# Moving transposes from TensorE to DMA in an attention and mixture-of-adapters kernel

## The chip, the cores and the metric

The kernel runs on one core of one Trainium2 chip. The metric is the device time of one execution in microseconds (us). Of three runs the median was 380.7 us (380.69 to 381.25).

## The reference

Four images of 12,288 query rows attend to a pooled and projected key/value set of 768 rows each (a 4 x 4 mean over a 384 x 32 grid). The output of the attention, 49,152 rows of 128, goes through a mixture of eight rank-16 adapters of which each row takes the best two.

```python
kv_pool = kv.reshape(B, H // r, r, W // r, r, C).mean(axis=(2, 4))
k = v = kv_pool.reshape(B, -1, C) @ w_sr
a = softmax(q @ k.T / sqrt(C))
x = (a @ v).reshape(-1, 128)
logits = x @ w_gate                  # 8 per row, the two largest are kept
w = softmax(the two largest)
out = x + sum over the two e of w[e] * (x @ A[e]) @ B[e]
```

## The kernel before, in words

**Chunks and slots.** The rows are cut into 96 chunks of 512 (24 to a batch). A chunk has six key tiles of 128 keys. Its life: `scores` (line 286) makes three units of two key tiles, each two 512-column matmuls into PSUM (`sg`, two buffers) and one exp on ScalarE into `em` (line 294). `attend` (line 296) multiplies `em` with the values, 24 matmuls into `acc`. `normalize` (line 313) divides on VectorE and leaves the rows x in `xn` (line 320). `top` and `route` (lines 335, 344) find the two best adapters, the latter on GpSimd, mostly for two chunks at once; `gates` (line 363) makes their weights with a tanh on ScalarE. `down` (line 412) multiplies the transposed x with all A, `gate` (line 417) weights the result into `hg` on VectorE, `up` (line 426) multiplies the transposed hg with all B, and `finish` (line 431) adds x and sends the output from SyncE's queue.

A slot is one turn of the loop at line 547. In slot k the scores of chunk k are made, chunk k-1 is attended, chunk k-2 is normalized, and older chunks go through down, gate and up. Everything is recorded in program order by `keep`, so that each engine, and SyncE's queue of DMAs, takes its instructions in the order of the source.

**Two ways of transposing.** `transposes` (line 371) uses TensorE: four 128 x 128 transposes of x, four of hg, into a PSUM bank `tt_ps`, then a copy to `tts` on VectorE (line 389). For chunks 68 to 89 (`by_dma`, line 328) it is done by DMA: `narrow` (line 402) copies x as bf16 into a strip on GpSimd, `gate` writes hg into the other half of the strip, and `turn_dma` (line 405) transposes both halves with one DMA inside SBUF from SyncE's queue. A chunk turned that way has two slots of flight. The strips lie in a tile of the pool of key rows that is free by then.

**The other DMAs.** q is cast to bf16 by a DMA from DRAM to DRAM on GpSimd's queue (`cast_q`, line 78) and then transposed by DMA from DRAM to SBUF on SyncE's queue (`load_qT`, line 83), 2048 rows at a time. `load_kv` (line 95) loads the rows of the next batch's key tiles, twelve DMAs of 512 KB to a batch, one in each of the first twelve slots of a batch. The additions that pool them run on GpSimd (line 223, 1.27 us each), three at a time in every second slot; nine steps `keys`, `values` and `turn` (from line 233) then make the keys and values on TensorE and VectorE. `begin` (line 468) issues the DMAs of a slot.

Of the kernel before, what the change touches and what calls it, by code (L numbers as in the profile page):

```python
# [20 lines left out]
def kernel(  # L21
# [33 lines left out]
    ppool = ctx.enter_context(tc.tile_pool(name="ppool", bufs=8))  # L55
# [20 lines left out]
    q_bf, qT, kvr, spare = {}, {}, {}, {}  # L76
# [6 lines left out]
    def load_qT(g):  # L83
        if g < B * NG - GC:
            t = qpool.tile([P, GT], BF16, tag="qT", name="qT")
        else:
            if "q" not in spare:
                spare["q"] = kvpool.tile([P, 4, 2, 4 * C], FP32, tag="kvr", name="qTs")
            t = spare["q"][:, g % GC].rearrange("p x c -> p (x c)").bitcast(BF16)
        keep(nc.sync.dma_start(t.rearrange("c (j p) -> c j p", p=P),  # L90
                               q_bf[g].rearrange("(p j) c -> p (j c)", p=P), transpose=True))
        qT[g] = t
# [109 lines left out]

    ring = [xpool.tile([P, 2, S, C + E], FP32, tag=f"xr{i}", name="xn") for i in range(6)]
# [82 lines left out]
    def scores(k, r):  # L286
        b = k // NB
        if k not in em:
            em[k] = ppool.tile([P, J, T], FP16, tag="em", name="em")
# [36 lines left out]
    SOLO, TURN = NCHUNK - 6, NCHUNK - 28  # L326
    sizes = [1, 1] + [2] * (TURN // 2 - 1) + [1] * (NCHUNK - TURN)
    by_dma = range(TURN, SOLO)
    first, size = {}, {}
# [65 lines left out]
    def strip(t, i):  # L395
        if "t" not in spare:
            t_ = kvpool.tile([P, 4, 2, 4 * C], FP32, tag="kvr", name="turn")
            spare["t"] = t_.rearrange("p r x c -> p (r x c)").bitcast(BF16).rearrange(
                "p (n t h s c) -> p n t h s c", n=4, t=2, h=2, s=S)
        return spare["t"][:, t % 4, i]  # L400
# [4 lines left out]
    def turn_dma(t, *what):  # L405
        lo, hi = (0 if what[0][0] is xT or len(what) == 2 else 1), (2 if what[-1][0] is hgT else 1)
        keep(nc.sync.dma_start(strip(t, 1)[:, lo:hi].rearrange("c h s p -> c (h s) p"),
                               strip(t, 0)[:, lo:hi].rearrange("p h s c -> p (h s c)"), transpose=True))
        for i, (d, k) in enumerate(what):
            d[k] = strip(t, 1)[:, lo + i]  # L410
# [52 lines left out]
    casts = sorted([k for k in range(8, 61, GC)] + [15, 19, 23, 39, 43, 47])  # L463
    loads = {4 * g - 6: g for g in range(4, 18)}
    loads.update({61: 20, 63: 21, 64: 18, 65: 22, 66: 19, 67: 23})
    assert len(casts) == B * NG - 4

    def begin(k):
        nonlocal sums, rest
        b, i = divmod(k, NB)  # L470
        g = k // GC
        if k in loads:
            load_qT(loads[k])
        if k in casts:
            cast_q(4 + casts.index(k))
        if b + 1 < B:
            lo = 3 if b == 0 else 0
            if i == lo:
                sums, rest = prepare(b + 1, nc.gpsimd)
                sums = sum(sums, [])  # L480
            if lo <= i < 12 + lo:
                load_kv(b + 1, (i - lo) // 4, (i - lo) % 4, None)
        if k == 7:
            for _ in range(2):
                sums.pop(0)()
# [10 lines left out]
    ready = {k: normed[first[k] + size[k] - 1] + 1 + (k in by_dma[:-1]) for k in range(NCHUNK)}  # L496
    enter, t, left = {}, 1, list(range(NCHUNK - 3))
    while left:
        can = [k for k in left if ready[k] <= t]
        enter[t] = can[:2] if t == SOLO + 2 else can[:1]  # L500
        left = [k for k in left if k not in enter[t]]
        t += 1
# [44 lines left out]
    for k in range(k1, NCHUNK):  # L547
        b, i = divmod(k, NB)
        ka = att.get(k, [])
        kx = enter.get(k, [])  # L550
        begin(k)
# [6 lines left out]
        kn = [n for n in att.get(k - 1, []) if normed[n] == k]  # L558
        unit()
        if kx and not kd and all(x_ in by_dma for x_ in kx):  # L560
            down(kx[0])
            todo = []
            for n in kn:
                normalize(n)
                if n in by_dma:
                    narrow(n, k)
                    todo = [(xT, n)]
            tanhs()
            for h_ in kh:
                if h_ not in by_dma:  # L570
                    transposes(None, h_, nc.vector)
# [3 lines left out]
            if len(kx) == 1:  # L575
                turn_dma(k, *todo)
            for u_ in ku:
                up(u_)
                finish(u_)
            attend(ka[0], 0)  # L580
            attend(ka[0], 1)
            unit()
            for n in kn:
                after_norm(n)
            attend(ka[0], 2)
            for x_ in kx[1:]:
                down(x_)
                gate(x_, strip(k, 0)[:, 0])
                turn_dma(k, (hgT, x_), *todo)
            attend(ka[0], 3)  # L590
            kh, ku = kx, kh
            continue
        tanhs()
        for x_ in kd:
            down(x_)
        for n in kn:
            normalize(n)
            if n in by_dma:
                narrow(n, k)
                turn_dma(k, (xT, n))  # L600
        px, ph = ([c for c in ks if c not in by_dma] for ks in (kx, kh))
        pairs = [(px[j] if j < len(px) else None, ph[j] if j < len(ph) else None)
                 for j in range(max(len(px), len(ph)))]
        for x_, h_ in pairs[:1]:
            transposes(x_, h_, nc.vector)
        for x_ in kd:
            gate(x_)
        unit()
        for u_ in ku:
            up(u_)  # L610
            finish(u_)
        for a_ in ka[:-1]:
            for s in range(S):
                attend(a_, s)
            normalize(a_)
            after_norm(a_)
        if ka and len(ka) == 1:
            attend(ka[0], 0)
        for n in kn:
            after_norm(n)  # L620
        if k >= 13:
            unit()
            n0 = 1
        else:
            attend(ka[0], 1)
            n0 = 2
        for x_ in kx[:1]:
            down(x_)
            gate(x_)
        kd = []  # L630
        if rest and i in ((14, 15, 16, 18, 19, 20, 21, 22, 23) if b == 0 else (11, 12, 13, 17, 18, 19, 21, 22, 23)):
            rest.pop(0)()
        for a_ in ka[-1:]:
            for s in range(n0 if len(ka) == 1 else 0, S):
                if s == S - 1:
                    for x_, h_ in pairs[1:]:
                        transposes(x_, h_, nc.scalar)
                        kd = [x_] if x_ is not None else []
                attend(a_, s)
        ku = kh  # L640
        kh = kx[:1] + kdone
        kdone = kd
        if b + 1 < B and i % 2 == 0 and (8 if b == 0 else 6) <= i <= 20:
            for _ in range(4 if (b, i) == (0, 18) else 3):
                sums.pop(0)()
# [185 lines left out]
```

## Time and profile before

| what | value |
|---|---|
| profiled execution, time | 380.87 us |
| its span | 379.1 us |
| mean granted clock of TensorE | 0.995 |
| instructions | 11473 |
| DMA packets, bytes | 93863, 82.22 MB |
| share of the 16 DMA engines' span, queue of SyncE (q1) | 69.8% |
| outputs: DMAs, size, median to landing | 94, 256 KB, 4.3 us |
| key rows | 45, 512 KB, 7.8 us |
| casts of q | 22, 512 KB, 7.7 us |
| turns of x and hg | 23, 3.1 us |
| transposes of q | 18, 7.4 us (and 4 more into another tile, 6.6 us) |

The page gives the busy time of each engine (PE is TensorE's matmuls, PEld its weight loads, DVE is VectorE, ACT ScalarE, POOL GpSimd, SP SyncE), then the span in 40 slices with a digit for the busy tenths, then the DMA queues, then the chain of work that ended last. Matmuls are pipelined, so the durations of single ones overlap, and sums over groups of them are more than their time.

### The profile page before, as it was taken

What the parts mean: (1) busy time and instruction counts of PE and PEld (TensorE: products, weight loads), DVE (VectorE), ACT (ScalarE), POOL (GpSimd) and SP (SyncE); (2) the same over time, 40 slices, a digit from 0 to 9 for tenths busy, and PEclk for the clock granted to TensorE, in tenths of its full rate; (3) what the DMA queues carried; (4) which work ended last, traced back from release to release, by engine and by line L of the source; (5) the groups of instructions that cost most, each with busy time, mean ns of one, the idle gap of its engine ahead of it and who ended that gap; (6) DMA issues with size and microseconds to landing.
All of it is one profiled execution on the core that took longest, in us unless ns stands there. A gap on an engine that the chain in (4) does not pass through costs nothing.

```text
span 379.1 us, 11473 instructions
## 1 busy us (share of the span) xinstructions
PE 368.8 (97%) x4448; PEld 292.5 (77%) x4448; DVE 307.6 (81%) x925; ACT 293.3 (77%) x368; POOL 217.8 (57%) x493
## 2 busy tenths in 40 slices
PE   8899999999999999999999999999999999999993
PEld 5577788788788887878788887878787777777782
DVE  1447799998989889898989888898988777777785
ACT  1448986776878788787878787777778999999873
POOL 0120468878732387777833267777675666666442
PEclk9999999999999999999999999999999999999998
DMA  7988979999999998997898998989955867777623
GB/s 247 388 291 151 279 184 266 340 224 241 152 213 228 299 278 268 255 235 165 171 201 226 288 239 245 306 233 198 217 137 140 169 163 153 150 205 168 141 86 140
DMA packets 93863, 82.22 MB, mean 217 GB/s; under 512 B 73104, under 2 KB 73872, under 8 KB 93456
## 3 DMA queue, kind: packets, MB, share of 16 engines
q1 hardware_dynamic: 92672, 69.75, 69.8%
q0 software_dynamic: 704, 11.54, 17.0%
q8 instruction: 35, 0.57, 0.6%
q10 hardware_dynamic: 432, 0.20, 0.2%
q14 instruction: 20, 0.16, 0.2%
HBM read 50.53 MB, written 36.70 MB: 230 GB/s over the span
## 4 chain that ended last, share of the span: by engine, by line
PE 91%; DMA 4%; DVE 2%; issue 1%; ACT 1%; SPq 0%; POOL 0%; ACTq 0%; DVEq 0%; POOLq 0%
PE acc L69 35%; PE sg L69 32%; PE tt_ps L69 8%; PE d_ps L69 5%; PE h_ps L69 5%; DMA kvr<-in_kv_dram 4%; PE kpT_ps L69 2%; PE v_ps L69 1%; DVE kvr L135 1%; DVE xn L320 1%; PE kfT_ps L69 1%; DMA out_dram<-osb 1%; PE qT_ps L69 0%; SPq L102 0%; PE tail_ps L69 0%
## 5 line engine op out<-in xcount | busy, mean ns | idle before, releaser
L294 ACT ACTIVATE em<-sg 128x1024 f16<-128x1024 f32 x288 | 282.4, 1022 | 66.8 <-PE sg L69 64.1
L69 PE MATMUL acc<-vx,em 128*128 128x136 f16 x2280 | 166.5, 223 | 0.0
L69 PEld LDWEIGHTS <-em 128*128 128x128 f16 x2304 | 145.2, 98 | 7.7 <-DVE xn L320 0.4
L69 PE MATMUL sg<-qT,kfT 128*128 128x512 bf16 x480 | 142.1, 379 | 0.8 <-ACT em L294 0.7
L320 DVE TENSOR_TENSOR xn<-acc,rinv 128x540 f32<-128x540 f32 x95 | 68.4, 720 | 3.3
L69 PEld LDWEIGHTS <-tts 128*128 128x128 bf16 x564 | 43.0, 98 | 31.6 <-issue 0.4
L223 POOL TENSOR_TENSOR kvr<-kvr 128x512 f32<-128x512 f32 x54 | 67.3, 1270 | 0.1
L352 POOL TENSOR_TENSOR over<-xn,srt 128x64 f32<-128x64 f32 (+1 forms) x120 | 30.9, 278 | 55.4 <-DVE srt L340 55.3
L433 DVE TENSOR_TENSOR osb<-d_ps,xn 128x512 f32<-128x512 f32 x91 | 62.5, 688 | 0.0
L420 DVE TENSOR_TENSOR hg<-h_ps,gw 128x512 bf16<-128x512 f32 x71 | 49.0, 691 | 6.3 <-POOL gw L368 1.2
L389 DVE COPY tts<-tt_ps 128x1024 bf16<-128x1024 bf16 (+1 forms) x73 | 49.0, 672 | 0.0
L69 PEld LDWEIGHTS <-kfT 128*128 128x128 bf16 x576 | 45.3, 98 | 2.7 <-issue 1.0
L315 DVE RECIPROCAL rinv<-acc 128x4 f32<-128x4 f32 x95 | 17.3, 182 | 36.9 <-PE acc L69 35.9
L367 POOL TENSOR_TENSOR gw<-th,over 128x64 f32<-128x64 f32 (+1 forms) x60 | 17.3, 288 | 49.6 <-ACT th L365 47.4
L69 PEld LDWEIGHTS <-xn 128*128 128x128 bf16 x296 | 22.5, 98 | 16.7 <-DVE xn L320 0.4
L340 DVE MAX8 srt<-xn 128x8 f32<-128x8 f32 x380 | 34.4, 152 | 0.1
L69 PE MATMUL sg<-qTs,kfT 128*128 128x512 bf16 x96 | 28.6, 379 | 0.0
L69 PE MATMUL tt_ps<-id_bf,xn 128*128 128x128 bf16 x284 | 27.4, 219 | 0.0
L69 PE MATMUL h_ps<-a_bf,tts 128*128 128x128 bf16 x284 | 27.4, 219 | 0.0
L69 PE MATMUL tt_ps<-id_bf,hg 128*128 128x128 bf16 x280 | 27.1, 219 | 0.0
L69 PE MATMUL d_ps<-b_bf,tts 128*128 128x128 bf16 x276 | 26.7, 219 | 0.1
L358 POOL TENSOR_SCALAR over<-over 128x64 f32<-128x64 f32 (+1 forms) x60 | 19.8, 330 | 5.4
(93 smaller groups left out, 280.7 us busy)
## 6 DMA issues: line engine op xcount, KB each, us to landing
out_dram<-osb SPq DMA_DIRECT2D x94, 256.0 KB, 4.3
kvr<-in_kv_dram SPq DMA_DIRECT2D x45, 512.0 KB, 7.8
qbf<-in_q_dram POOLq DMA_DIRECT2D x22, 512.0 KB, 7.7
qf<-in_q_dram SPq DMA_DIRECT2D x8, 256.0 KB, 7.4
kvr<-in_kv_dram SPq DMA_DIRECT2D x6, 256.0 KB, 7.8
out_dram<-osb SPq DMA_DIRECT2D x3, 128.0 KB, 2.3
turn<-turn SPq DMA_TRANSPOSE x23, 3.1
qT<-qbf SPq DMA_TRANSPOSE x18, 7.4
```

Source lines behind the costliest of these rows:

```text
L69: return keep(nc.tensor.matmul(*a, **k))
L223: keep(adder.tensor_tensor(u[:, lo:hi], u[:, lo:hi], v[:, lo:hi], op=ALU.add))
L294: keep(nc.scalar.activation(em[k][:, 2 * r:2 * r + 2], ps, AF.Exp, bias=0.0, scale=scale))
L315: keep(nc.vector.reciprocal(ri, acc[k][:, :, VC]))
L320: keep(nc.vector.tensor_tensor(x[:, :, 0:VC], acc[k][:, :, 0:VC], ri.unsqueeze(2).broadcast_to([P, S, VC]), op=ALU.mult))
L340: keep(nc.vector.max(srt[k0][:, m, s], xn[k][:, s, C:C + E]))
L352: keep(eng.tensor_tensor(d, lg, so[:, :, i].unsqueeze(2).broadcast_to([P, n, 8]), op=ALU.subtract))
L358: keep(eng.tensor_scalar(mask, mask, 0.0, None, op0=ALU.is_ge))
L367: keep(eng.tensor_tensor(w[:, 0:n], th, mask, op=ALU.mult))
L389: keep(nc.vector.tensor_copy(sb[:, lo:hi], ps[:, lo:hi]))
L420: keep(nc.vector.tensor_tensor(hg[k].rearrange("p s (e r) -> p (s e) r", e=E), hp[k].rearrange("p s (e r) -> p (s e) r", e=E), gw[k0][:, m ...
L433: keep(nc.vector.tensor_tensor(osb, dp[k], xn[k][:, :, 0:C], op=ALU.add))
```

## The change

`by_dma` now begins at chunk 12 instead of 68. From there on hg is always transposed by DMA. x is transposed by DMA for chunks 20, 22, ... 60 and for 62 to 89; for chunks 12 to 19 and the odd ones from 21 to 61 (`x_by_pe`) it is still done on TensorE, one slot before it is used (`turn_next`), with the copy on ScalarE for chunks 13, 17, 21, ... 61 and on VectorE for the others. A chunk under 80 enters `down` five slots after its own slot and `up` three slots after that (three slots of flight), later ones as before (two slots). Pairs of chunks are routed together up to chunk 79 instead of 67.

The tiles of `em` are eight fixed ones; from chunk 13 on only the first four are used for `em`, and the strips lie in the other four: four strips as source, eight as destination. The key rows of batches 2 and 3 are loaded one in every second slot, their additions run one in each slot over 24 slots, and the steps that make keys and values follow behind them. Casts and transposes of q have new slots.

```diff
-    ppool = ctx.enter_context(tc.tile_pool(name="ppool", bufs=8))
...
     def load_qT(g):
-        if g < B * NG - GC:
-            t = qpool.tile([P, GT], BF16, tag="qT", name="qT")
-        else:
-            if "q" not in spare:
-                spare["q"] = kvpool.tile([P, 4, 2, 4 * C], FP32, tag="kvr", name="qTs")
-            t = spare["q"][:, g % GC].rearrange("p x c -> p (x c)").bitcast(BF16)
+        t = qpool.tile([P, GT], BF16, tag="qT", name="qT")
...
+    ems = [xpool.tile([P, J, T], FP16, tag=f"em{i}", name="em") for i in range(8)]
...
-            em[k] = ppool.tile([P, J, T], FP16, tag="em", name="em")
+            em[k] = ems[k % 8 if k < TURN + 1 else k % 4]
...
-    SOLO, TURN = NCHUNK - 6, NCHUNK - 28
-    sizes = [1, 1] + [2] * (TURN // 2 - 1) + [1] * (NCHUNK - TURN)
+    SOLO, TURN, NEAR = NCHUNK - 6, 12, NCHUNK - 16
+    sizes = [1, 1] + [2] * (NEAR // 2 - 1) + [1] * (NCHUNK - NEAR)
     by_dma = range(TURN, SOLO)
+    x_by_pe = [*range(TURN, 20), *range(21, NEAR - 18, 2)]
...
     def strip(t, i):
-        if "t" not in spare:
-            t_ = kvpool.tile([P, 4, 2, 4 * C], FP32, tag="kvr", name="turn")
...
+        n = 4 + t % 8 if i else t % 4
+        v = ems[4 + n // 3].rearrange("p j t -> p (j t)").bitcast(BF16)
+        return v[:, n % 3 * 2 * T:(n % 3 + 1) * 2 * T].rearrange("p (h s c) -> p h s c", h=2, s=S)
...
-    def turn_dma(t, *what):
-        lo, hi = (0 if what[0][0] is xT or len(what) == 2 else 1), (2 if what[-1][0] is hgT else 1)
-        keep(nc.sync.dma_start(strip(t, 1)[:, lo:hi].rearrange("c h s p -> c (h s) p"),
+    def turn_dma(t, u, *what):
+        lo = 0 if what[0][0] is xT else 1
+        hi = lo + len(what)
+        keep(nc.sync.dma_start(strip(u, 1)[:, lo:hi].rearrange("c h s p -> c (h s) p"),
                                strip(t, 0)[:, lo:hi].rearrange("p h s c -> p (h s c)"), transpose=True))
...
-    casts = sorted([k for k in range(8, 61, GC)] + [15, 19, 23, 39, 43, 47])
-    loads = {4 * g - 6: g for g in range(4, 18)}
-    loads.update({61: 20, 63: 21, 64: 18, 65: 22, 66: 19, 67: 23})
+    casts = {4 * g - 8: g for g in range(4, 19)}
+    casts.update({67: 19, 70: 20, 73: 21, 76: 22, 79: 23})
+    loads = {4 * g - 5: g for g in range(4, 20)}
+    loads.update({74: 20, 77: 21, 80: 22, 82: 23})
+    rows_at = {3 + n: (1, n) for n in range(12)}
+    rows_at.update({NB * b - 32 + 2 * n: (b, n) for b in (2, 3) for n in range(12)})
+    adds_at = {7: 2, 8: 3, 10: 3, 12: 3, 14: 3, 16: 3, 18: 4, 20: 3}
+    adds_at.update({k: 1 for k in range(NB - 3, 3 * NB - 3)})
+    keys_at = [14, 15, 16, 18, 19, 20, 22, 23, 23] + [
+        NB * b - 24 + n for b in (2, 3) for n in (5, 6, 7, 13, 14, 15, 21, 22, 23)]
...
-    ready = {k: normed[first[k] + size[k] - 1] + 1 + (k in by_dma[:-1]) for k in range(NCHUNK)}
...
+    enter, ups = {}, {}
+    for k in range(NCHUNK - 3):
+        slow = 1 if k < NEAR else 0
+        if k not in by_dma:
+            t = max(normed[first[k] + size[k] - 1] + 1, max(enter, default=0) + 1 if k < TURN else 0)
+        else:
+            t = min(k + 4 + slow, SOLO + 2)
+            ups.setdefault(t + 2 + slow, []).append(k)
+        enter.setdefault(t, []).append(k)
...
+        def new_x(n):
+            normalize(n)
+            if n in by_dma and n not in x_by_pe:
+                narrow(n, k)
+                return [(xT, n)]
+            return []
+
+        def turn_next(k):
+            for x_ in enter.get(k + 1, []):
+                if x_ in x_by_pe:
+                    transposes(x_, None, nc.scalar if x_ % 4 == 1 else nc.vector)
+
         unit()
-        if kx and not kd and all(x_ in by_dma for x_ in kx):
+        if kx and kx[0] in by_dma:
             down(kx[0])
-            todo = []
-            for n in kn:
-                normalize(n)
-                if n in by_dma:
-                    narrow(n, k)
-                    todo = [(xT, n)]
+            todo = new_x(kn)
             tanhs()
             for h_ in kh:
-                if h_ not in by_dma:
-                    transposes(None, h_, nc.vector)
+                transposes(None, h_, nc.vector)
             unit()
             gate(kx[0], strip(k, 0)[:, 1])
             todo.append((hgT, kx[0]))
-            if len(kx) == 1:
-                turn_dma(k, *todo)
-            for u_ in ku:
+            turn_dma(k, k, *todo)
+            for u_ in ku + ups.get(k, []):
                 up(u_)
                 finish(u_)
-            attend(ka[0], 0)
-            attend(ka[0], 1)
+            attend(ka, 0)
+            attend(ka, 1)
+            turn_next(k)
             unit()
-            for n in kn:
-                after_norm(n)
-            attend(ka[0], 2)
+            after_norm(kn)
+            for _ in range(keys_at.count(k)):
+                rest.pop(0)()
+            attend(ka, 2)
             for x_ in kx[1:]:
                 down(x_)
-                gate(x_, strip(k, 0)[:, 0])
-                turn_dma(k, (hgT, x_), *todo)
-            attend(ka[0], 3)
+                gate(x_, strip(k + 2, 0)[:, 1])
+                turn_dma(k + 2, k + 4, (hgT, x_))
+            attend(ka, 3)
...
+        add(k)
```

## The prediction

> **What bounds the kernel now.** I read the page's busy row and slices first, then the chain, then the DMA queues, then single slots. One slot is one chunk's turn through the loop (lines 547 to 645).
>
> ```profile
> PE 368.8 (97%) x4448; PEld 292.5 (77%) x4448; DVE 307.6 (81%) x925; ACT 293.3 (77%) x368; POOL 217.8 (57%) x493
> PE   8899999999999999999999999999999999999993
> DMA  7988979999999998997898998989955867777623
> PE 91%; DMA 4%; DVE 2%; issue 1%; ACT 1%; SPq 0%; POOL 0%; ACTq 0%; DVEq 0%; POOLq 0%
> q0 software_dynamic: 704, 11.54, 17.0%
> ```
>
> TensorE ends the chain and is full from slice 2 to the end, so every matmul removed is time, until something else is late. The DMA row says what that could be: nearly full up to slice 29 and three quarters after.
>
> The price of a slot is the distance between two reciprocals (line 315, one per chunk). In the timeline of VectorE two plain slots stand 3.61 us apart in the middle, and 3.16 us apart in the late stage where chunks 68 to 89 are already turned by DMA:
>
> ```profile
> 127.56 0.18 DVE L315 RECIPROCAL rinv<-acc 128x4 f32<-128x4 f32 x1 [0.30 <-PE acc L69]
> 131.17 0.18 DVE L315 RECIPROCAL rinv<-acc 128x4 f32<-128x4 f32 x1 [0.38 <-PE acc L69]
> ...
> 320.20 0.18 DVE L315 RECIPROCAL rinv<-acc 128x4 f32<-128x4 f32 x1 [0.75 <-PE acc L69]
> 323.37 0.18 DVE L315 RECIPROCAL rinv<-acc 128x4 f32<-128x4 f32 x1 [0.75 <-PE acc L69]
> ```
>
> The two kinds of slot differ by eight transposes (four of x, four of hg): 0.45 us, so a group of four costs 0.225 us. The late stage also shows the next engine. ScalarE is gapless there, three exps in 3.04 us and a tanh:
>
> ```profile
> 318.51 3.15 ACT L294 ACTIVATE em<-sg 128x1024 f16<-128x1024 f32 x3
> 321.55 0.22 ACT L365 ACTIVATE th<-over 128x32 f32<-128x32 f32 x1
> 321.67 3.15 ACT L294 ACTIVATE em<-sg 128x1024 f16<-128x1024 f32 x3
> ```
>
> **What leaves TensorE.** Chunks 12 to 67 lose their hg group (56). Of x, chunks 20, 22, ... 60 and 62 to 67 are new by DMA (27). That is 83 groups, or 332 matmuls, and the instructions of the changed kernel, listed by engine, have 332 fewer. 83 x 0.225 = 18.7 us; the profiled time 380.87 (span 379.1 and 1.77 around it; the median of the three runs is 380.7) would become **362.2** if nothing else were late. The summed busy time of the two transpose rows would say more, but those durations overlap (219 ns each), so I use the slot distance.
>
> **What the other engines do.** ScalarE per four slots: 12 exps 12.16, two pair tanhs about 0.3, and one copy of a transposed x (13 in all; nearest row 585 ns, line 673) give 13.0 us, against TensorE's 2 x 3.16 + 2 x 3.385 = 13.09. It fits with nothing to spare; the score buffers in PSUM (two) cover the uneven slot. If they don't, 13 x 0.585 = 7.6 us is the most it costs, and a smoother order gains nothing since TensorE stays behind it; I take 0. VectorE does less: its copies of 1024 columns (0.69) shrink to 16 of 512 (0.42). GpSimd gains 27 narrow copies (610 ns, 16.5 us) at 57% busy. Its additions come one per slot at 1.27 us, so a narrow copy can wait for at most one addition, and the DMA behind it is 1.3 us later: inside the slack below. Key rows follow their last addition by half a slot or more; I take 0 for the six groups in batches 2 and 3, at most 1.3 us each if GpSimd slips a slot. The three slots of flight cost nothing on TensorE: they change only which chunk stands in a slot.
>
> **What DMA must carry.** Four views of one microsecond give prices: plain transfers (kv rows, outputs), a transpose inside SBUF, a transpose of q from DRAM, and one that begins badly (two microseconds):
>
> ```profile
> DMA packets 116, 0.39 MB, mean 389 GB/s; under 512 B 8, under 2 KB 8, under 8 KB 116
> ...
> DMA packets 827, 0.21 MB, mean 212 GB/s; under 512 B 827, under 2 KB 827, under 8 KB 827
> ...
> DMA packets 1124, 0.29 MB, mean 288 GB/s; under 512 B 1124, under 2 KB 1124, under 8 KB 1124
> ...
> DMA packets 598, 0.25 MB, mean 127 GB/s; under 512 B 549, under 2 KB 549, under 8 KB 598
> ```
>
> All packets are 256 B in a transpose. So on all 16 engines: an output (0.262 MB at 389 GB/s) 0.67 us; a kv row 1.35; a 128x512 transpose (512 packets at 827 per us) 0.62; a qT (2048 at 1124) 1.82; a cast of q 17.0% x 379.1 / 22 = 2.93.
>
> Slots 22 to 62 of the new order (hg always, x every second, one kv row every second, one qT and one cast every fourth), per four slots: 4 x 0.62 + 2 x 0.62 + 4 x 0.67 + 2 x 1.35 + 1.82 + 2.93 = 13.85, or **3.47 us a slot**. TensorE needs 3.27 a slot there (half at 3.16, half at 3.385), and each key group adds about 0.85 (before, three slots of a group took 3.84, 4.12, 3.72): 41 x 3.27 + 5 x 0.85 = 138.4 us, or 3.38 a slot. DMA is the longer one.
>
> That sum supposes engines that never stand still. How far from it they are is bounded by the kernel before: with a kv row in every slot it carried 0.67 + 1.35 + (1.82 + 2.93) / 4 = 3.21 a slot in 3.61, and TensorE wasn't held up. So the stretch lies between 1.00 and 3.61 / 3.21 = 1.125. The last view above shows where it comes from: 127 GB/s at the start of a transpose. I take the middle, 1.06: two thirds of the new load is of kinds that ran undisturbed in the late stage, one third (qT, cast) of the kind that stretches. 3.47 x 1.06 = 3.68.
>
> Some lag is free. A turn is issued 1.85 us into its slot (320.0 to 321.85), lands 3.1 later, and is now needed 0.43 into the third slot after: 3 x 3.38 + 0.43 - 1.85 - 3.1 = 5.6 us of slack, or 4.3 with a kv row (1.35) queued before it. So slots 22 to 62 take 41 x 3.68 - 4.3 = 146.6, 8.2 more than TensorE's 138.4. Slots 63 to 82 (no kv, x always): (8 x 0.62 + 4 x 0.67 + 1.82 + 2.93) / 4 = 3.10, x 1.06 = 3.29, 65.8 against TensorE's 20 x 3.16 + 0.85 + 0.45 = 64.5: 1.3 more. Behind slot 82 there is slack as before.
>
> Sum: 362.2 + 8.2 + 1.3 = **371.7 us**, faster by 2.4%. With no stretch it is 362.2; with 1.125, 41 x 3.90 - 142.7 = 17.2 and 20 x 3.49 - 64.5 = 5.3 give 384.7.
>
> [...]
>
> **Rivals.**
> 1. *DMA hides it all: 362.2 (chance 0.20 for under 364.5).* For it: 3.47 lies only 0.09 above TensorE's 3.38, and 4.3 us of lag covers 41 x 0.09. Against it: the DMA row is already full at a lower load.
> 2. *Partial: DMA becomes the bound by a little, 364.5 to 380.1 (0.55).* My forecast.
> 3. *Slower: casts on transposes.* [...] Before, transposes were 1.8 of 14.4 us of four slots; now 5.5 of 13.5, and one cast comes in each four. If that brings the stretch over f, with 41 x 3.47 f + 20 x 3.10 f = 204.3 f against 207.2 + 18.7, the gain is eaten at f = 1.106, or **3.84 us a slot**. At 1.125 it is 384.7 (0.20 for over 381.6).
> 4. *SyncE's queue.* It is in order, and a q transpose holds it longest:
>
> ```profile
> 130.26 6.24 SPq L90 DMA_TRANSPOSE qT<-qbf  x1
> 321.85 1.24 SPq L407 DMA_TRANSPOSE turn<-turn  x1
> ```
>
> Per four slots: two turns at 1.24, two of half the size at about 0.62, outputs 4 x 0.53, rows 2 x 0.55, a qT at 6.24, and eleven gaps of 0.09: 14.2, or 3.55 a slot; 41 x 3.55 - 142.7 = 2.9, so 365. It lies inside rival 2.
>
> That the change doesn't move the transposes is excluded by the count of instructions.
>
> **Numbers.** A measurement of this kernel tells about 0.2% from no change. Faster 0.75, within 0.2% 0.05, slower 0.20. The range 361 to 383 leaves out some 0.03 below (a smoother DMA also moves nothing under TensorE's sum) and some 0.13 above.
>
> **What would show it.** Right: slots of about 3.16 and 3.39 in turn where DMA keeps up; TensorE under 95% busy, with waits of h_ps or d_ps matmuls for DMA em<-em in slots 22 to 62, 8 us or so in all; the late stage unchanged at 3.16. Rival 1: TensorE still full, no such waits. Rival 3: these waits over 18 us, turns landing 10 us or more after issue, and mean slots over 3.84. Wrong altogether: ScalarE's copies or GpSimd's additions as the last releaser before TensorE.

## The result, and the profile after

The changed kernel took 420.64 us (median of four runs, 414.91 to 426.52) against 380.98 us (380.69 to 381.35): slower, by a ratio of 1.0916 with a 95% interval of 1.0867 to 1.0965. The ratio lies under that of the medians because two of the four runs of the changed kernel were disturbed and are left out of it. Forecast were 371.7 us and a range of 361 to 383, so it was wrong in size and in sign. The profiled execution took 416.88 us with a span of 415.1.

These lines of the page of the changed kernel answer to those of before: busy time, slices, the chain, two groups of matmuls with the idle time ahead of them (the last two numbers are idle time and its main releaser), and two rows of DMA issues (the last number is the median from issue to landing).

```profile
PE 362.8 (87%) x4116; PEld 278.8 (67%) x4116; DVE 275.2 (66%) x885; ACT 304.7 (73%) x375; POOL 227.0 (55%) x484
...
PE   8899999999989868878799877978886997999993
...
PEclk9999999999999999998979999999998898999998
DMA  8989699999999989999999999999999989986623
...
PE 49%; DMA 28%; POOL 9%; DVE 7%; issue 3%; SPq 1%; ACT 1%; POOLq 0%; DVEq 0%; ACTq 0%
...
L68 PE MATMUL h_ps<-a_bf,em 128*128 128x128 bf16 x196 | 19.5, 223 | 30.0 <-DMA em<-em 30.0
L68 PE MATMUL d_ps<-b_bf,em 128*128 128x128 bf16 x312 | 30.9, 223 | 10.7 <-DMA em<-em 9.9
...
em<-em SPq DMA_TRANSPOSE x78, 4.8
...
qT<-qbf SPq DMA_TRANSPOSE x22, 8.0
```

TensorE is 87% busy after 97%, and works 362.8 us where it worked 368.8. The matmuls h_ps and d_ps, which read what the turns deliver, now wait 39.9 us for a DMA, where the kernel before had no such wait worth a line, and DMA holds 28% of the chain (4% before). The DMA row is full from slice 7 to 34, bar two. The clock row shows 7 or 8 in five slices ahead of the last.

Where the time went, by stages of slots. A stage is the distance between two reciprocals in the timeline of VectorE; the half clock is the time in it for which the trace grants 0.5.

| slots | before | forecast | after | half clock in it |
|---|---|---|---|---|
| 12 to 21 | 37.7 | | 35.8 | 0 |
| 22 to 62 | 152.1 | 146.6 | 175.4 | 10.2 |
| 63 to 82 | 69.6 | 65.8 | 80.9 | 10.2 |
| 83 to 96 | 45.5 | as before | 48.8 | 0 |

Time comes in steps. Two plain slots of 3.61 and 3.62 us and a long one of 9.49, in the timeline of VectorE:

```profile
196.57 0.18 DVE L310 RECIPROCAL rinv<-acc 128x4 f32<-128x4 f32 x1 [0.75 <-PE acc L68]
...
200.18 0.18 DVE L310 RECIPROCAL rinv<-acc 128x4 f32<-128x4 f32 x1 [0.29 <-PE acc L68]
...
203.80 0.18 DVE L310 RECIPROCAL rinv<-acc 128x4 f32<-128x4 f32 x1
...
213.29 0.18 DVE L310 RECIPROCAL rinv<-acc 128x4 f32<-128x4 f32 x1 [1.07 <-PE acc L68]
```

In the long one TensorE stands until a turn has landed. SyncE's queue and TensorE around it (the second number of a line is how long the instruction held its engine; the bracket is the idle time before):

```profile
196.41 4.29 SPq L402 DMA_TRANSPOSE em<-em  x1
200.80 2.29 SPq L429 DMA_DIRECT2D out_dram<-osb  x1
```

```profile
203.60 0.59 PE L68 MATMUL sg<-qT,kfT 128*128 128x512 bf16 x2
207.15 0.61 PE L68 MATMUL h_ps<-a_bf,em 128*128 128x128 bf16 x4 [2.96 <-DMA em<-em]
```

The turn issued at 196.41 landed at 207.1, 10.7 us later. The records of the DMA's packets say what it waited for. A cast begins at 196.84 in 16 packets of 32 KB, which I read as one to an engine. Fifteen end by 200.46; the sixteenth began only at 198.72, took 4.23 us and ended at 202.95. Eight packets of a key row, queued ahead of the turn, then follow one another from 202.93 to 204.19, one at a time (the records don't name engines; one at a time, behind the late packet, I read as that engine). Twenty packets of the turn that began at 202.2 to 202.5, by the same reading on other engines, stand for 1.9 to 2.2 us and end together at 204.42 to 204.45. From 202.5 to 204.2 the DMA view of the profile has next to nothing starting (its first row is in tenths again, for 40 slices of this stretch):

```profile
DMA  0000000000200020020002000200200020002000
...
DMA packets 11, 0.03 MB, mean 19 GB/s; under 512 B 3, under 2 KB 3, under 8 KB 11
```

So, by that reading, the other engines held packets of the transpose and waited for the one that was behind. A second stand, of 1.35 us, follows at 206.0, after a single packet of 16 KB of instructions from 204.87 to 206.01. Behind it comes a loss that the forecast did not have. The windows of the same place (length, busy time of the five engines, then the granted clock, the DMA share and GB/s):

```profile
203.00:207.00 4.00, 1.19 (x15) 0.70 (x12) 1.61 (x4) 1.73 (x2) 1.21 (x1) 0.92 0.96 145
207.00:209.00 2.00, 1.85 (x12) 1.30 (x13) 0.69 (x1) 0.29 (x1) 0.00 (x0) 0.50 0.89 323
...
211.00:213.00 2.00, 2.00 (x16) 1.68 (x15) 0.93 (x6) 1.02 (x1) 1.12 (x4) 0.50 1.23 286
213.00:215.00 2.00, 2.00 (x25) 1.52 (x23) 1.68 (x4) 1.21 (x3) 1.99 (x4) 0.96 0.82 210
```

After its 2.96 us of standing, TensorE runs at half clock for 6.8 us. Such stretches add up to 20.5 us before the tail. An estimate from that, with half the work done at half the clock: they cost at most half of it, 10.2 us.

### The profile page after: what moved, and what is told of

It is laid out like the page before. It is cut to its first block, busy times and chain, and to the rows that moved or that the text cites. A ratio compares the mean times of both kernels' runs of the same rounds, so it can differ in the third digit from the quotient of the medians.

```text
span 415.1 us, 11084 instructions
## 1 busy us (share of the span) xinstructions
PE 362.8 (87%) x4116; PEld 278.8 (67%) x4116; DVE 275.2 (66%) x885; ACT 304.7 (73%) x375; POOL 227.0 (55%) x484
## 4 chain that ended last, share of the span: by engine, by line
PE 49%; DMA 28%; POOL 9%; DVE 7%; issue 3%; SPq 1%; ACT 1%; POOLq 0%; DVEq 0%; ACTq 0%
DMA em<-em 23%; PE acc L68 21%; PE sg L68 17%; PE h_ps L68 4%; DMA kvr<-in_kv_dram 4%; PE d_ps L68 3%; POOL kvr L218 3%; PE tt_ps L68 3%; DVE em L415 2%; POOL over L348 2%; DMA qf<-in_q_dram 2%; DVE osb L428 1%; POOL em L397 1%; POOL over L353 1%; DVE srt L336 1%
## 5 line engine op out<-in xcount | busy, mean ns | idle before, releaser
L289 ACT ACTIVATE em<-sg 128x1024 f16<-128x1024 f32 x288 | 288.6, 1024 | 91.6 <-PE sg L68 85.5
L68 PEld LDWEIGHTS <-em 128*128 128x128 f16 (+1 forms) x2812 | 185.3, 100 | 93.6 <-DMA em<-em 51.1
L68 PE MATMUL sg<-qT,kfT 128*128 128x512 bf16 x576 | 174.1, 385 | 0.8 <-ACT em L289 0.7
L415 DVE TENSOR_TENSOR em<-h_ps,gw 128x512 bf16<-128x512 f32 x78 | 53.3, 683 | 31.3 <-PE h_ps L68 30.0
L397 POOL CAST em<-xn 128x512 bf16<-128x512 f32 x49 | 29.9, 611 | 31.1 <-DVE xn L315 31.0
L68 PE MATMUL h_ps<-a_bf,em 128*128 128x128 bf16 x196 | 19.5, 223 | 30.0 <-DMA em<-em 30.0
L68 PE MATMUL d_ps<-b_bf,em 128*128 128x128 bf16 x312 | 30.9, 223 | 10.7 <-DMA em<-em 9.9
L68 PEld LDWEIGHTS <-tts 128*128 128x128 bf16 x232 | 17.5, 98 | 11.8
L354 POOL TENSOR_SCALAR over<-over 128x64 f32<-128x64 f32 (+1 forms) x54 | 18.7, 347 | 4.9
L385 DVE COPY tts<-tt_ps 128x512 bf16<-128x512 bf16 (+1 forms) x33 | 17.1, 519 | 6.3 <-PE tt_ps L68 5.8
L364 POOL TENSOR_TENSOR gw<-gw,over 128x64 f32<-128x64 f32 (+1 forms) x54 | 16.3, 302 | 4.2
L216 POOL TENSOR_TENSOR kvr<-kvr 128x512 f32<-128x512 f32 (+1 forms) x18 | 18.0, 999 | 0.4
```

Source lines behind the costliest of these rows:

```text
L68: return keep(nc.tensor.matmul(*a, **k))
L216: keep(adder.tensor_tensor(u, u, v, op=ALU.add))
L289: keep(nc.scalar.activation(em[k][:, 2 * r:2 * r + 2], ps, AF.Exp, bias=0.0, scale=scale))
L354: keep(eng.tensor_scalar(mask, mask, 0.0, None, op0=ALU.is_ge))
L397: keep(nc.gpsimd.tensor_copy(strip(t, 0)[:, 0], xn[k][:, :, 0:C]))
L415: keep(nc.vector.tensor_tensor(hg[k].rearrange("p s (e r) -> p (s e) r", e=E), hp[k].rearrange("p s (e r) -> p (s e) r", e=E), gw[k0][:, m ...
```

## The experiments

Unless a line says otherwise each kernel is the changed one with one edit, and its time is the median of its runs, with that of the kernel before on the same chip at 380.5 to 380.8 us. "Net" is a stage less half of its time at half clock. A single profile stands behind each stage, and executions of the changed kernel differ by some us, so a few us of a stage tell nothing.

**No casts.** The casts of the loop are left out; two of the casts made ahead of it serve instead, so wrong rows of q are used.

```diff
-            cast_q(casts[k])
+            q_bf[casts[k]] = q_bf[2 + casts[k] % 2]
```

> The changed kernel without the casts of q of groups 4 to 23 (their transposes read the bf16 rows of groups 2 and 3; left out: 20 DMAs of 2.93 us on all engines, and the right q). Theory A, too many bytes for the 16 DMA engines: four slots lose 2.93 us of load times a stretch of 1.2, 0.88 us a slot, so slots of 4.28 fall to TensorE's 3.38 and the time to 372 to 380. Theory B, SyncE's queue in order and held: the holds of outputs and turns that follow a cast (2.7 to 4.3 us instead of 0.53 and 1.24) go, about 2.5 us in 16.7, so 385 to 390. Theory C, bursts longer than three slots of flight: the burst of cast and q transpose is cut, so 365 to 375. If a cast costs only its own 2.93 / 4 a slot and no wait, 390.

Measured: 368.11 us (367.73 to 368.5), 0.9672 (0.9623 to 0.9722) of the kernel before. Page and waits:

```profile
PE 346.9 (95%) x4049; PEld 274.4 (75%) x4116; DVE 272.5 (75%) x885; ACT 303.0 (83%) x375; POOL 216.1 (59%) x464
...
PEclk9999999999999999999999999999999999999997
DMA  7989968997799999999999999999999999966523
...
em<-em SPq DMA_TRANSPOSE x78, 4.0
```

```profile
PEld L68 <- DMA em<-em: 6.5, 6, 1.8
```

The waits for turns shrink from 51.1 us of weight loads to 6.5, and the clock never drops before the tail. Slots 22 to 62 take 143.6 us and 63 to 82 take 64.6, where the forecast had TensorE's own need at 138.4 and 64.5. All turns are still there. The stalls need the casts. The time lies in the range of theory C, under those of A and B. The DMA row is as full as with the casts: it counts the time that packets take, and packets that stand count too (a share of 1.56 at 207 GB/s from 199.5 to 202.5 us of the changed kernel, where the twenty shown above begin), so a full row does not tell that the engines have no room.

**Four slots of flight** up to chunk 75.

```diff
-        slow = 1 if k < NEAR else 0
+        slow = 2 if k < NEAR - 4 else 1 if k < NEAR else 0
```

> The changed kernel with four slots of flight instead of three for chunks 12 to 75. Turns land 12.5 us after their slot's reciprocal, now against 13.5 us of flight instead of 10. Theories A and B (a rate that does not suffice, on the engines or on SyncE's queue): the backlog only grows by one slot more and the time stays within 5 us of 417. Theory C (bursts): the stalls of 42 us nearly vanish, 370 to 380.

Measured: 433.76 us (424.55 and 442.97). Slots 22 to 62 net 167.4 against 170.3, slots 63 to 82 83.5 against 75.8. More slack buys nothing, so a turn is not merely late now and then, and theory C is out.

**All x by TensorE** in slots 22 to 62, so that no turn there has more than the 512 packets of hg.

```diff
-    x_by_pe = [*range(TURN, 20), *range(21, NEAR - 18, 2)]
+    x_by_pe = [*range(TURN, NEAR - 18)]
```

> The changed kernel with x of chunks 20, 22, ... 60 on TensorE again; each slot still has one turn, of half the size. TensorE gets 21 groups more, 4.7 us. Theory A: the load of four slots falls by 1.24 of 13.85, 9%, 0.38 a slot, 15 us in all: about 400. Theory B: SyncE is held as long by half a turn (1.21 us) as by a whole one (1.25), so the time does not fall: 413 to 422. Theory C: between, 405 to 415.

Measured: 420.69 us (416.83 and 424.55); slots 22 to 62 net 167.4. A third of the packets of that stage's turns went, at the same number of turns, and nearly nothing came of it, though TensorE had 4.7 us more to do there by the forecast's price. Theory A's 400 is out.

**Key rows of batches 2 and 3 from GpSimd's queue.**

```diff
-            keep(nc.sync.dma_start(kvr[b, h][:, r].rearrange("p g c -> p (g c)"), src))
+            queue = nc.gpsimd if b > 1 else nc.sync
+            keep(queue.dma_start(kvr[b, h][:, r].rearrange("p g c -> p (g c)"), src))
```

> The changed kernel with the key rows of batches 2 and 3 issued from GpSimd's queue instead of SyncE's; the same bytes on the same engines. Theory A: no change, 413 to 422. Theory B: SyncE loses two issues in four slots, 1.3 to 2.2 us of 16.7, 0.33 to 0.55 a slot over 41 slots: 395 to 404. GpSimd gets 0.29 us a slot more and may pass them on to the turns: up to 5 us against both.

Measured: 421.22 us, ratio 1.1068 (1.0807 to 1.1329). The median from issue to landing of a turn rose from 4.8 to 6.5 us. With two issues in four slots taken from SyncE nothing is gained, so theory B's 395 to 404 is out: SyncE's full queue shows a backlog that it does not make.

**x and hg in two DMAs** where one carried both, up to slot 62: 21 transposes more, the same bytes.

```diff
-            turn_dma(k, k, *todo)
+            for what in ([[w_] for w_ in todo] if k < 63 else [todo]):
+                turn_dma(k, k, *what)
```

> The changed kernel with x and hg of a slot in two DMAs of half the size up to slot 62, where one DMA carried both: the same bytes, two more transposes in every four slots. Theory A by bytes: no change, 412 to 424. Theory F, each transpose costs a fixed time beside its bytes (on the engines, about 0.42 us of packets that wait for the slowest engine; on SyncE 1.3 us of hold and gap): 0.8 to 2.6 us more in 16.6, 0.2 to 0.65 a slot over 41 slots, so 425 to 443.

Measured: 436.37 us (433.02 and 439.71). Slots 22 to 62 net 177.2: 6.9 more for 21 transposes, an estimate of 0.33 us each, and 17 us more at half clock. The profile is of the execution of 439.71 us, so the split is rough; that the time rises, as theory F has it, both executions show.

**Turns from chunk 68 only**, as before the change; the spread of key rows and additions stays.

```diff
-    SOLO, TURN, NEAR = NCHUNK - 6, 12, NCHUNK - 16
+    SOLO, TURN, NEAR = NCHUNK - 6, NCHUNK - 28, NCHUNK - 16
...
-    x_by_pe = [*range(TURN, 20), *range(21, NEAR - 18, 2)]
+    x_by_pe = []
```

> The changed kernel with x and hg of chunks 12 to 67 on TensorE as before, so what is left of the change is the spread of key rows, additions and key steps, the slots of the casts and transposes of q, and three slots of flight for chunks 68 to 79. If the added turns alone cost the time (theories A and F): 380 to 388, the excess from slots 73 to 82, where turns now meet casts and transposes of q (0.7 us a slot there in the changed kernel). If the new places of rows or casts cost it: over 395.

Measured: 396.3 us, ratio 1.0408 (1.0338 to 1.0478). Slots 22 to 62 take 154.1 us, 2 more than before: the spread does no harm worth the name. The loss is in slots 63 to 82, 76.4 against 69.6, where turns now meet casts, and in 83 to 96, 51.7 against 45.5.

**Half the turns**: hg by DMA in every second chunk up to 61 only, x by TensorE there. The hg that is still turned there has one slot of flight more.

```diff
-    x_by_pe = [*range(TURN, 20), *range(21, NEAR - 18, 2)]
+    x_by_pe = [*range(TURN, NEAR - 18)]
+    h_by_pe = range(TURN + 1, NEAR - 18, 2)
...
-            ups.setdefault(t + 2 + slow, []).append(k)
+            if k not in h_by_pe:
+                ups.setdefault(t + 2 + slow + (k < NEAR - 18), []).append(k)
...
-            gate(kx[0], strip(k, 0)[:, 1])
-            todo.append((hgT, kx[0]))
-            turn_dma(k, k, *todo)
+            if kx[0] in h_by_pe:
+                gate(kx[0])
+            else:
+                gate(kx[0], strip(k, 0)[:, 1])
+                todo.append((hgT, kx[0]))
+            if todo:
+                turn_dma(k, k, *todo)
...
-            kh, ku = [], kh
+            kh, ku = [x_ for x_ in kx if x_ in h_by_pe], kh
```

> The changed kernel with hg by DMA for every second chunk only up to 61 (the others on TensorE) and x on TensorE up to 61: two turns of 128x512 in four slots instead of four turns. TensorE needs 3.50 a slot there, 3.60 with key steps. Theory A: 13.85 - 2.48 = 11.4 a four slots, times the stretch of 1.20 that was measured, is 13.7 against TensorE's 14.0, so the stalls of slots 22 to 62 go and those of 63 to 82 stay: 386 to 394. If a cast on any transpose is what costs (theory C'), one cast of 3 us still meets them in every four slots: over 400.

Measured: 398.63 us, ratio 1.0469 (1.0363 to 1.0575). Slots 22 to 62 take 154.5 us with no half clock, 16 less net than with a turn in each slot and still 2 over the kernel before; slots 63 to 82, unchanged, take 81.6. The time lies between what theory A and theory C' forecast.

**No key rows** for batches 2 and 3: 24 loads of 512 KB left out, wrong keys used.

```diff
-            load_kv(b, n // 4, n % 4, None)
+            if b == 1:
+                load_kv(b, n // 4, n % 4, None)
+            else:
+                kvr[b, n // 4] = kvr[1, n // 4]
```

> The changed kernel without the key rows of batches 2 and 3 (their additions and key steps run on the tiles of batch 1; left out: 24 DMAs of 512 KB, and the right keys). It takes 2.70 us from the load of four slots in 22 to 62, about what the casts were there (2.93), while casts and transposes stay. Theory A: as without casts in these slots, 3.4 a slot, and 12 us of stalls left behind slot 62: 378 to 386. Theory C', the casts are special since they hold single engines while a transpose needs all: most stalls stay, 395 to 410.

Measured: 411.75 us, ratio 1.0814 (1.0768 to 1.0859). The waits stay:

```profile
PE d_ps L68 <- DMA em<-em: 18.2, 7, 5.1
PE h_ps L68 <- DMA em<-em: 15.1, 6, 4.1
```

By the prices of the forecast, rows are 2.70 and a cast 2.93 us of four slots. Without rows the stage wins 9.6 us net, without casts 26.7. By bytes they should be near each other, so theory A is out; the time is a little over the range of C'.

**Small packets in the casts**: the same bytes to 128 rows with a gap between them. And the same in the kernel before.

```diff
-        t = qdram.tile([GT, C], BF16, tag=f"q{g}", name=f"qbf{g}")
-        keep(nc.gpsimd.dma_start(t, q[g // NG, (g % NG) * GT:(g % NG + 1) * GT]))
+        t = qdram.tile([P, GT + 64], BF16, tag=f"q{g}", name=f"qbf{g}")[:, 0:GT]
+        keep(nc.gpsimd.dma_start(t, q[g // NG, (g % NG) * GT:(g % NG + 1) * GT]
+                                 .rearrange("(p j) c -> p (j c)", p=P)))
...
-                               q_bf[g].rearrange("(p j) c -> p (j c)", p=P), transpose=True))
+                               q_bf[g], transpose=True))
```

> The changed kernel with the same 512 KB casted, but written to 128 rows with a gap between them, so that a cast should be cut into some 128 packets of 4 KB (2048 elements) in place of 16 of 32 KB, one to an engine. Nothing is left out. Lockstep (a transpose needs its engines together, and one engine that is held by a cast's long packet holds the rest): an engine is held for some 0.3 us at a time in place of 2.4, so the long stalls every four slots go, and with them the stretches of half the clock: 370 to 390 us, above the 368 of the kernel without casts, since the bytes are still carried. Bytes only (the engines are simply full): the same bytes in more packets, so no gain, 410 us or more. If the packets do not become smaller, the time stays at 415 to 427 and the trace shows 32 KB packets still.

> The control: the kernel before with the same small packets in its casts. Nothing is left out. Both theories: TensorE sets the time there and turns are few while casts run, so 380 to 382 us. If small packets cost the engines more in all, it shows here as a longer time, over 383.

Measured: 404.88 us (396.88 to 406.19), and for the kernel before 380.47, ratio 1.0001 (0.9991 to 1.001). The packets of GpSimd's queue rose from 704 to 3168:

```profile
q0 software_dynamic: 3168, 11.54, 18.5%
```

Some 16 us of 52 are gained by the medians, 18 by the fastest executions (396.88 against 414.91), so lockstep as put there fell in its size, and bytes alone (410 or more) too. The standing itself is still to be seen. From 284.18 eighteen packets of a transpose stand for up to 2.1 us, while the last four 4 KB packets of a cast follow one another, one each 0.4 us, to 286.01, as on one engine. All eighteen end at 286.27 to 286.30. The DMA view of 284.5 to 286 has those four and four more packets, and no start of the transpose at all:

```profile
DMA  5000000010500000001005000000010500000001
...
DMA packets 8, 0.02 MB, mean 16 GB/s; under 512 B 0, under 2 KB 0, under 8 KB 8
```

**Plain copies in place of casts**, 1 MB from DRAM to DRAM, from SyncE's queue or from GpSimd's. The casts are left out as in the first experiment.

```diff
-            cast_q(casts[k])
+            copy_q(casts[k])
...
+    def copy_q(g):
+        t = qdram.tile([P, GT + 64], FP32, tag=f"q{g}", name=f"qcopy{g}")[:, 0:GT]
+        keep(nc.sync.dma_start(t, q[g // NG, (g % NG) * GT:(g % NG + 1) * GT]
+                                 .rearrange("(p j) c -> p (j c)", p=P)))
+        q_bf[g] = q_bf[2 + g % 2]
```

The second has `nc.gpsimd` in the place of `nc.sync`.

> The changed kernel with each of the 20 casts of its loop replaced by a plain copy of the same 1 MB of q from DRAM to DRAM, some 2.7 us of all engines at 389 GB/s, issued from SyncE's queue, in which the transposes are too. Left out: the casts themselves; wrong q rows are used. Own queue (a transpose is held where another queue's packets lie between its own): in one queue the packets come in order and do not mix, so most of the gain of leaving out the casts stays: 370 to 390 us. Bytes: 400 us or more, and the same as the copy from GpSimd's queue. The cast as such (the conversion): 370 to 390 here and there.

> The same plain copies as in e11_copy_same_queue, issued from GpSimd's queue, as the casts were. Left out: the casts themselves; wrong q rows are used. Own queue: the transposes are held as by the casts, 400 us or more, at least 15 us above the copy in SyncE's queue. Bytes: the same time as there. The cast as such: 370 to 390 us.

Measured: 412.08 us (1.083, 1.0771 to 1.0889) from SyncE's queue and 400.43 us (1.0524, 1.0464 to 1.0584) from GpSimd's. The waits of the first, then of the second:

```profile
PE h_ps L68 <- DMA em<-em: 34.6, 19, 3.8
```

```profile
PE h_ps L68 <- DMA em<-em: 19.9, 11, 4.2
PE d_ps L68 <- DMA em<-em: 6.6, 5, 1.8
```

Neither the conversion nor the second queue is what costs: a plain copy brings the stalls back, and in the transposes' own queue more of them. What is left of the three is the expectation "400 us or more" for plain bytes; its "same time" did not hold: the two queues differ by 12 us, and no run shows why.

**Casts in halves**, two DMAs two slots apart.

```diff
...
-            cast_q(casts[k])
+            cast_q(casts[k], 1)
+        if k + 2 in casts:
+            cast_q(casts[k + 2], 0)
```

> The changed kernel with each cast in two DMAs of 256 KB each, the first half two slots earlier. Nothing is left out; bytes and queue are the same, a burst is half as long. Burst (a cast holds the transposes for longer than the free lag of some 4 us): stalls go, 395 us or less. Sum of bytes: 410 to 425 us as the changed kernel.

Measured: 416.92 us (416.34 and 417.5), ratio 1.0954 (1.0932 to 1.0976). That is what the sum of bytes forecast; the length of one burst is not it.

**Casts ahead of the turns.** Four kernels with all casts before, or nearly before, the turns; nothing is left out.

```diff
-    casts = {4 * g - 8: g for g in range(4, 19)}
-    casts.update({67: 19, 70: 20, 73: 21, 76: 22, 79: 23})
+    casts = {2 * g: g for g in range(4, 24)}
```

This is one cast in every second slot from 8 to 46, with turns from chunk 48 or from 68 (`TURN`, and `x_by_pe` empty).

> Nothing is left out. The casts come in every second slot from 8 to 46, the turns by DMA begin at chunk 48, and x is then always turned by DMA. If casts are what holds the turns, no stall stays: 40 groups of four transposes fewer than before on TensorE at 0.225 us are 9 us, and one key group more or less does not matter: 371 to 375 us, faster than before. If the turns beside the key rows of batch 3 (slots 40 to 62) are too much by bytes or by SyncE's queue: 380 us or more.

> Nothing is left out. As e6_turns_from_68 (396.3 us), but the casts come in every second slot from 8 to 46, ahead of all turns by DMA. If casts that meet turns are the cause of its long slots 75 to 87: 380 to 383 us, as before the change. If the spread key rows or three slots of flight there are the cause: 390 us or more.

Turns from 48: 394.07 us, of eleven executions three at 380.3 to 381.9, as the kernel before (ratio 1.0007), and eight at 389.4 to 404.3; the profile is of the one at 389.37. Turns from 68: 402.37 us, ratio 1.0575 (1.0552 to 1.0598). As totals the expectations for casts as the cause, 371 to 375 and 380 to 383, both failed. By stages the second splits cleanly. Its slots 63 to 82 take 68.1 us where the kernel that differs from it in the casts' slots alone takes 76.4 (73.0 net). What it loses lies in slots 12 to 62, 207.4 against 191.5: there, beside two casts and two key rows in four slots, the transposes of q come late. TensorE's wait for them, from 68 and then from 48:

```profile
PE sg L68 <- DMA qT<-qbf: 10.0, 3, 7.3
```

```profile
PE sg L68 <- DMA qT<-qbf: 7.3, 1, 7.3
```

The next two thin the casts out, to every two and a half slots with turns from chunk 56 and to every third with turns from 64, both with the small packets above and `x_by_pe` empty (`casts = {8 + 5 * (g - 4) // 2: g ...}` and `{3 * g - 4: g ...}`).

> Nothing is left out. Casts every two and a half slots from 8 to 55, in packets of 4 KB as in e9_small_casts; turns by DMA, x too, from chunk 56, so that no cast is issued once they run. 24 groups of four transposes fewer than before at 0.225 us: 5.4 us, 375 to 376.5 us if no stall stays. If casts crowd the key rows as in e13 (an early stall on the transposes of q): 380 us or more, uneven from run to run.

> Nothing is left out. Casts every third slot from 8 to 65, in packets of 4 KB; turns by DMA from chunk 64. 8 groups fewer than before: 1.8 us, 378.5 to 379.5 us if no stall stays; the last cast is the only one near the first turns. 380 us or more if key rows spread over two slots each are what holds the transposes of q.

At two and a half: 393.68 us (386.32 to 402.36). The profile, of the execution of 402.36 us, has long slots before 62 again, and 64.0 us in slots 63 to 82, TensorE's own need. At three: 382.39 us, ratio 1.0071 (1.0034 to 1.0108), no stall of TensorE over 2 us and no half clock before the tail; 63 to 82 take 68.3, but 83 to 96 take 50.1. Both missed the gain that they were to show (375 to 376.5 and 378.5 to 379.5).

The last is the kernel with turns from 64 and two slots of flight throughout; the edit is against that kernel.

```diff
-    SOLO, TURN, NEAR = NCHUNK - 6, 64, NCHUNK - 16
+    SOLO, TURN, NEAR = NCHUNK - 6, 64, 64
```

> As e16_turns_from_64 (382.4 us), but all turns have two slots of flight and each chunk is routed alone from 64 on, as the kernel before has it from 68 on, so there is no slot in which the flight gets shorter. Nothing is left out. If that step is what slots 83 to 96 pay for: they take 46 us in place of 50, and the whole 378 to 379, less than before. If it is the last transposes of q (slots 74 to 82, in the kernel before by slot 67): the same 382 or more, or waits in slots 64 to 82.

Measured: 383.39 us, ratio 1.0069 (1.0047 to 1.0091). Slots 83 to 96 take 47.2, 2.9 less. That the step from three slots of flight to two costs this much is not shown: kernels with that step take from 47.4 (no key rows) to 53.6 (four slots) there. One slot, in which a turn comes behind a late transpose of q, takes 7.24, and nothing is won. No version that computes the reference beat the kernel before.

## Why the prediction was wrong

- **83 groups leave TensorE, 18.7 us: right.** Without casts the changed kernel takes 368.1 us and its plain slots return to 3.16 and 3.38; its late stage takes 64.6 us against a need forecast at 64.5, slots 22 to 62 take 143.6 against 138.4, with some waits for turns left.
- **"The stretch lies between 1.00 and 3.61 / 3.21 = 1.125 ... I take the middle, 1.06": this is the step that failed.** Slots 22 to 62 took 175.4 us; with the 4.3 of free lag that is 179.7 / (41 x 3.47) = 1.26, or 1.23 net of half clock. The bound came from a kernel that had no turns in that stage. It bounded that mix, and nothing bounded the new one, in which turns run beside casts: without the casts the same stage takes 143.6 us, 26.7 less net.
- **The prices in that sum were too low too.** From first to last packet, between slots 12 and 85, a turn of 1024 packets took some 1.87 us on average, one of 512 1.07 and a qT 2.71 (without casts about 1.7, 1.1 and 2.8, so it is not the casts that make them dear); less what other packets carried meanwhile (0.41, 0.53, 0.31) 1.46, 0.54 and 2.40, against 1.24, 0.62 and 1.82. A cast's 2.93 us of engine time (2.86 measured) was spread over 3.84 from first start to last end. Per four slots of 22 to 62: 2 x 1.46 + 2 x 0.54 + 2.40 + 4 x 0.67 + 2 x 1.35 + 3.84 = 15.6, or 3.91 a slot and 41 x 3.91 - 4.3 = 156 us; of 63 to 82: 4 x 1.46 + 2.40 + 2.68 + 3.84 = 14.8, 73.8 us. Net measured are 170.3 and 75.8. So measured prices explain the late stage to 2 us, and 9 of the 24 us by which the other passes its forecast of 146.6.
- **Rival 1, and "the DMA row is already full" against it.** The rival is out, but that row was no argument: it is as full in the kernel without casts, which hardly waits.
- **"Some lag is free": no.** SyncE was all but gapless (its DMA instructions held it for 163.3 of the 175.4 us of slots 22 to 62), and in slots 22 to 62 a turn was issued mostly 6 to 9 us into its slot (median 7.3; without casts 3.7), not 1.85, so the lag was spent before it began. A slot more of it (four slots of flight) didn't help.
- **Rival 3, casts on transposes (0.20): the right place, the wrong price.** Its signs came: waits over 18 us (39.9), mean slots over 3.84 (4.28). Only one turn landed after 10 us (10.7); the median was 4.8. It gave 384.7, since it took the same bound of 1.125. Over the twelve kernels with five casts or copies in slots 63 to 82 that stage takes 73.0 to 83.5 us net; over the eight with none, or with one in slot 65, 64.0 to 69.6. The wait of the other engines for the one that is behind shows in packet records (twenty packets that stand for 1.9 to 2.2 us), as far as these tell engines apart. But such standing, counted as the packets of transposes that took over 0.5 us between slots 12 and 85, comes to 36 us for each of 16 engines after, 29 without casts and 28 before, so it alone is not the difference of 49 us between the profiles with and without casts. That a cast holds all transposes for its 3.84 us where the engines have no room left fits the late stage; it is not shown.
- **Rival 4, SyncE's queue: a wrong term.** A turn of 512 packets held SyncE for 1.23 us (median of slots 22 to 62), about as one of 1024 (1.27), not 0.62. But relief of that queue brought nothing.
- **Half clock: missing**, up to 10.2 us of the 45.2 by which the profiled 416.88 passes the forecast. **"Behind slot 82 there is slack as before": wrong by 3.3 us**; what costs them is open.
- **ScalarE's copies and GpSimd's additions at nothing: right**; on the lists of waits the copies (`tts`) release no wait of TensorE, and the additions (`kvr`) 0.5 us.

Open: why a third fewer packets in the turns bring nearly nothing where half as many turns bring 16 us net; why key rows left out bring 9.6 us net and casts 26.7; and why smaller packets or plain copies in the casts' place cost a third to over a half less in slots 22 to 62 (158.6, 161.0 and 155.4 net against 170.3 with casts and 143.6 without) and no less in 63 to 82 (76.8, 80.5, 76.8; the figures with small packets are from its execution of 406.19 us). A cost for each transpose, whatever its size, would fit the first, with the 0.33 us of the split turns; the others are not settled. Casts and copies go from DRAM to DRAM and key rows do not; whether that is the difference, no run tells.

## What to carry to other kernels

A bound on a stretch that is read from a kernel holds for the mix of transfers in that kernel; where a change brings another kind beside them, run that pair first, or take the whole time of the other transfer as the price. Before moving work to DMA look at what shares the engines with it slot by slot: the same turns cost nothing where no cast ran (64.6 us) and 11 us where five did. And a stall of TensorE can have a second price behind it: four in the changed kernel, of 2.79 to 4.02 us, had half the clock behind them for 3.41 or 6.83 us.

## What the hardware showed that was not expected

- In each of the 20 traces every stretch of TensorE at a granted clock of 0.5 begins on one grid of 3.41 us, to 1 ns, and before the tail it lasts 3.41, 6.83 or 10.24 us. In the changed kernel the four before the tail begin at 189.26, 206.33, 318.97 and 346.27 us. Before the last 20 us of the traces, 62 windows of that grid at full clock are followed by half clock, and TensorE stands for 1.91 us or more in each; of the 2025 others only one has more than 2.0 (2.14). In the changed kernel it stands for 2.10 to 2.77 us in the four that are followed by half clock, and for 1.91 or less in the others behind its first matmul. So in these counts half clock went with how long TensorE stood within one window, and not with the length of a gap: behind gaps of 2.04 us (casts in halves) and 2.12 (late turns, early casts) it came, behind two of 3.0 us in the changed kernel, each with the edge of a window in it, it did not. The window of the gap of 2.96 us that was shown above, with 1.27 us of work and half clock behind it (columns as above), and then the fuller window of the gap of 3.05 us that begins at 239.2, with 1.62 us of work, and the one behind it:

```profile
202.92:206.33 3.41, 1.27 (x16) 0.78 (x13) 1.61 (x4) 1.81 (x2) 1.29 (x2) 1.00 1.10 167
...
240.47:243.88 3.41, 1.62 (x23) 1.39 (x24) 1.13 (x2) 0.70 (x1) 0.00 (x0) 1.00 1.23 231
243.88:247.29 3.41, 3.41 (x46) 2.70 (x44) 2.77 (x11) 2.62 (x5) 1.99 (x5) 1.00 1.18 325
```

- A transpose inside SBUF held SyncE for about as long with 512 packets as with 1024: 1.23 and 1.27 us, medians of slots 22 to 62 in the changed kernel.
- Packets of one transpose stood and ended together, 0.2 to 0.3 us after the last plain packet ahead of them: twenty in the changed kernel, for up to 2.2 us (204.19 and then 204.42 to 204.45), and eighteen with small casts, for up to 2.1 (286.01 and then 286.27 to 286.30). That they stood on other engines than the plain packet is read from their order.
- A cast from DRAM to DRAM of 512 KB written went out as 16 packets of 32 KB, 2.86 us each on average in the changed kernel; split into 4 KB it cost the kernel before nothing (1.0001).
